# The first 256 of 512 rows of x transposed by TensorE, the other 256 by a DMA transpose, with the first four groups of h computed in two halves

## The chip, the cores and the metric

The kernel runs on one core of a Trainium2 chip. The time is device microseconds from launch to end. The record also has each launch's span, from the first to the last instruction: most launches take 1.7 to 2 us more than it. One number is the median of several launches. Launches of one kernel differ by up to about a microsecond (in one of the jobs below, 11 launches of the same kernel lay between 320.51 and 321.78, their spans between 318.7 and 319.8), and the whole effect in question here is smaller than that. So much of the evidence is taken from single traces, by the place of single instructions.

## The reference

```python
# x: (1, 2048, 640), w1: (640, 1536), w2: (1536, 640), grad_out like x; all bfloat16
def forward(x, w1, w2):
    h = jnp.einsum("bsd,df->bsf", x, w1)
    h = jax.nn.silu(h)
    return jnp.einsum("bsf,fd->bsd", h, w2)
# outputs: the forward result and the gradients for x, w1 and w2
```

## The kernel before

The kernel goes through x in four chunks of 512 rows. For each chunk it computes h in 12 groups: a group is 128 columns of h, made by five matmuls (one for each 128 of the 640 columns of x) of 128 x 128 weights by 512 columns. Then come the output product, the product for grad_out and the gradient of x, and at the end the gradients of the weights. Only the head of the program, up to about 20 us, is touched by the change. There x must be transposed first: TensorE does it against an identity matrix, and VectorE and ScalarE copy the results out of PSUM.

```python
KM, NWARM, LAG_G = 2, 22, 4     # P = 128, SC = FC = 512, DT = 5, FT = 12, FB = 4, NFC = 3
...
for i in range(NWARM):          # keeps TensorE busy until x has landed
    early.append(nc.tensor.matmul(wp[:, 0:P], lhsT=warm[:], rhs=warm[:], start=True, stop=True))
...
early += [load_x_half(0), load_x_half(1), load_w1_rows(0, 1), load_w1_rows(1, KM)]
load_w1_rows(KM, DT)            # w1 rows of columns 0..511: "the first slice"
...
for fc in range(1, NFC):
    load_w1(fc * FC, (fc + 1) * FC)     # second and third slice, 640 KB each
...
nc.sync.dma_start(out=w2_nat[:], in_=w2_v[:])
goT_next = load_goT(0)                  # a DMA transpose

def pe_x_half(xT, half):
    lo = half * 2 * P
    for dt_ in range(DT):
        tp = ps_h.tile([P, 2, P], dt_in, name="tp", tag="hp")
        for q in range(2):
            nc.tensor.transpose(tp[:, q, :], x_two[:, half, q, dt_ * P:(dt_ + 1) * P], ident[:])
        copy = nc.scalar.copy if dt_ % 2 else nc.vector.tensor_copy
        copy(out=xT[:, dt_, lo:lo + 2 * P].rearrange("p (s q) -> p q s", q=2), in_=tp[:])

pe_x_half(xT_next, 0)
pe_x_half(xT_next, 1)
...
def h_first(xT, aT, ghT):       # the 12 groups of the first chunk
    hps = []
    for ft in range(FB):
        hps.append(ps_h.tile([P, SC], FP32, name="hp"))
    for dt_ in range(KM):
        for ft in range(FB):
            h_mm(hps[ft], ft, xT, dt_, dt_ + 1)
    for i in range(FT + LAG_G):
        if i < FT:
            if i < FB:
                h_mm(hps[i], i, xT, KM, DT)
            else:
                hps.append(ps_h.tile([P, SC], FP32, name="hp"))
                h_mm(hps[i], i, xT, 0, DT)
            silu_a(i, hps[i], aT)
        ...
```

All loads go through SyncE's one queue, in the order of the text. Groups 1 to 4 need the first w1 slice, groups 5 to 8 the second. I call the first group that needs the second slice "group 5".

## Time and profile before

| | before |
|---|---|
| median | 320.82 us (3 launches, 320.68 to 321.51) |
| span of the profiled launch | 319.4 us |
| TensorE (PE) busy | 314.6 us, 98% |
| transposes of x | 20, from 3.19 us, 107 ns apart |
| second w1 slice: issued, landed on the last engine | 2.48, 9.91 us |
| group 5's first matmul | 10.08 us |

First the line of engine times of the page of before: busy microseconds, share of the span, number of instructions.

```profile
PE 314.6 (98%) x1469; PEld 146.3 (46%) x1498; DVE 102.6 (32%) x182; ACT 77.9 (24%) x142; POOL 0.7 (0%) x6
```

PE has almost no idle time, so whatever the head saves or loses moves the end by as much. Next the timeline of before: PE from 3 to 12 us, then PEld (the weight loads) over the same stretch. The columns are start, length of the merged piece, engine, line, operation, tiles, shape and count; in brackets the idle time ahead and what ended it.

```profile
3.19 2.31 PE L197 MATMUL tp<-ident,x_two 128*128 128x128 bf16 x20 [0.16 <-DMA x_two<-in_x_dram]
5.30 6.02 PE L206 MATMUL hp<-xT,w_nat 128*128 128x512 bf16 x24
```

```profile
6.15 3.60 PEld L206 LDWEIGHTS <-w_nat 128*128 128x128 bf16 x17 [0.28 <-issue]
9.95 1.95 PEld L206 LDWEIGHTS <-w_nat 128*128 128x128 bf16 x10 [0.21 <-DMA w_nat<-in_w_dram]
```

PE has no break between the transposes and the twelfth microsecond. But the weight load at 9.95 is group 5's, and it waited 0.21 us for the second w1 slice. It waits ahead of its matmul, so PE itself lost nothing; yet the slice had only about 0.1 us to spare. Last the queue of SyncE (SPq) in the timeline of before (here the length is how long SyncE was busy issuing), and from the DMA view of 0 to 20 us the moved GB/s, a number for each half microsecond.

```profile
0.09 0.87 SPq L173 DMA_DIRECT2D x_two<-in_x_dram  x2
1.00 1.44 SPq L178 DMA_DIRECT2D w_nat<-in_w_dram  x3
2.48 1.06 SPq L169 DMA_DIRECT2D w_nat<-in_w_dram  x2
```

```profile
GB/s 0 0 82 266 374 374 351 366 289 358 358 336 324 324 348 371 374 379 376 380 366 366 358 364 364 364 366 344 271 133 62 26 23 83 292 289 319 152 28 39
```

The two w1 slices (L169) are issued at 2.48 us. From 2 to 14 us the queue moves about 350 GB/s almost without a gap.

### The profile page before, as it was taken

How to read it: one execution, taken by the hardware profiler on the slowest of the kernel's cores; microseconds unless marked ns; L12 is line 12 of the kernel's file. 1: busy time of each engine (PE TensorE's matmuls, PEld its weight loads, DVE VectorE, ACT ScalarE, POOL GpSimd, SP SyncE). 2: the span in 40 equal slices, each digit the busy share in tenths (PEclk: the TensorE clock that was granted, in tenths of full speed). 3: DMA queues.
4: the chain of work that ended last, by engine and by line, in shares of the span. 5: the costliest groups of instructions: out<-in, count | busy, mean ns of one | idle time of the engine just before them, and what ended most of it. 6: DMA issues, size and time to landing. Idle time of an engine off the chain costs nothing.

```text
span 319.4 us, 3541 instructions
## 1 busy us (share of the span) xinstructions
PE 314.6 (98%) x1469; PEld 146.3 (46%) x1498; DVE 102.6 (32%) x182; ACT 77.9 (24%) x142; POOL 0.7 (0%) x6
## 2 busy tenths in 40 slices
PE   9999999999999999999999999999999999999996
PEld 6444444444444444444444444444444444444443
DVE  3771541477410087710147741000000100001001
ACT  4960000545201254411054520110100001001100
POOL 0000000000000000000000000000000000000000
PEclk9999999999999999999999999999999999999999
DMA  8999999999999855292634079819999998995111
GB/s 282 307 180 222 246 292 264 341 263 292 293 278 271 223 190 140 86 308 76 171 114 133 2 259 267 217 30 294 265 212 257 267 240 292 253 294 182 49 37 45
DMA packets 147312, 67.33 MB, mean 211 GB/s; under 512 B 112609, under 2 KB 147041, under 8 KB 147297
## 3 DMA queue, kind: packets, MB, share of 16 engines
q1 hardware_dynamic: 147296, 67.12, 80.9%
q8 instruction: 11, 0.18, 0.2%
q14 instruction: 5, 0.03, 0.0%
HBM read 9.83 MB, written 28.97 MB: 121 GB/s over the span
## 4 chain that ended last, share of the span: by engine, by line
PE 98%; DMA 1%; issue 1%; DVE 0%; DVEq 0%; SPq 0%
PE hp L269 32%; PE hp L206 16%; PE hp L357 16%; PE hp L253 16%; PE hp L406 15%; PE hp L387 1%; DMA x_two<-in_x_dram 1%; PE tp L197 1%; DVE g L398 0%; DVEq L398 0%; SPq L434 0%
## 5 line engine op out<-in xcount | busy, mean ns | idle before, releaser
L206 PE MATMUL hp<-xT,w_nat 128*128 128x512 bf16 x238 | 57.2, 381 | 0.1
L253 PE MATMUL hp<-goT,w2T 128*128 128x512 bf16 x232 | 56.4, 379 | 0.4
L269 PE MATMUL hp<-aT,w_nat 128*128 128x512 bf16 x235 | 52.2, 379 | 0.3
L269 PE MATMUL hp<-ghT,w1T 128*128 128x512 bf16 x235 | 52.2, 379 | 0.3
L357 PE MATMUL hp<-a_blk,go_nat 128*128 128x512 bf16 x236 | 51.8, 379 | 0.2
L406 PE MATMUL hp<-gh_blk,x_nat 128*128 128x512 bf16 x219 | 48.2, 379 | 0.3
L277 ACT ACTIVATE oT<-hp 128x512 bf16<-128x512 f32 x24 | 14.3, 598 | 109.8 <-PE hp L269 109.8
L215 ACT ACTIVATE aT<-hp 128x512 bf16<-128x512 f32 x48 | 29.9, 625 | 33.0 <-PE hp L206 33.0
L206 PEld LDWEIGHTS <-w_nat 128*128 128x128 bf16 x240 | 23.6, 99 | 28.4 <-issue 0.6
L269 PEld LDWEIGHTS <-w1T 128*128 128x128 bf16 x240 | 23.5, 98 | 28.3
L357 PEld LDWEIGHTS <-go_nat 128*128 128x128 bf16 x240 | 23.5, 98 | 28.3
L253 PEld LDWEIGHTS <-w2T 128*128 128x128 bf16 x240 | 23.5, 98 | 28.3
L269 PEld LDWEIGHTS <-w_nat 128*128 128x128 bf16 x240 | 23.5, 98 | 28.4
L279 DVE CAST oT<-hp 128x512 bf16<-128x512 f32 x16 | 11.1, 692 | 77.0 <-PE hp L269 63.5
L260 DVE SCALAR_TENSOR_TENSOR ghT<-ghT,hp 128x512 bf16<-128x512 bf16 x48 | 32.5, 682 | 7.3 <-PE hp L253 7.3
L406 PEld LDWEIGHTS <-x_nat 128*128 128x128 bf16 x224 | 21.9, 98 | 26.4
L222 DVE SCALAR_TENSOR_TENSOR ghT<-aT,v 128x512 bf16<-128x512 bf16 x48 | 32.8, 687 | 0.5
L221 DVE TENSOR_SCALAR v<-t 128x512 bf16<-128x512 f32 x48 | 20.3, 426 | 30.5 <-ACT t L219 30.5
L219 ACT ACTIVATE t<-hp 128x512 f32<-128x512 f32 x48 | 29.8, 625 | 0.0
L417 DVE CAST g<-hp 128x512 bf16<-128x512 f32 x7 | 4.8, 692 | 47.0 <-PE hp L406 27.4
L367 DVE CAST g2T<-hp 128x512 bf16<-128x512 f32 x7 | 4.8, 692 | 46.1 <-PE hp L357 46.1
L365 ACT ACTIVATE g2T<-hp 128x512 bf16<-128x512 f32 x8 | 4.8, 597 | 47.0 <-PE hp L357 40.8
(20 smaller groups left out, 27.0 us busy)
## 6 DMA issues: line engine op xcount, KB each, us to landing
aT_scr<-aT SPq DMA_DIRECT2D x4, 1536.0 KB, 6.2
ghT_scr<-ghT SPq DMA_DIRECT2D x4, 1536.0 KB, 8.0
out_dram<-o_sb SPq DMA_DIRECT2D x8, 640.0 KB, 3.6
oT_scr<-oT SPq DMA_DIRECT2D x4, 640.0 KB, 3.6
go_nat<-in_grad_out_dram SPq DMA_DIRECT2D x4, 640.0 KB, 6.4
x_nat<-in_x_dram SPq DMA_DIRECT2D x4, 640.0 KB, 5.3
gxT_scr<-oT SPq DMA_DIRECT2D x4, 640.0 KB, 4.7
w_nat<-in_w_dram SPq DMA_DIRECT2D x1, 1920.0 KB, 13.4
```

The lines of the kernel that those rows point to most:

```text
L206: nc.tensor.matmul(hp[:], lhsT=w1_nat[:, dt_, ft * P:(ft + 1) * P], rhs=xT[:, dt_, :], start=(dt_ == 0), stop=(dt_ == DT - 1),)
L215: nc.scalar.activation(aT[:, ft, :], hp[:], ACT.Silu)
L219: nc.scalar.activation(t[:], hp[:], ACT.Tanh, scale=0.5)
L221: nc.vector.tensor_scalar(out=v[:], in0=t[:], scalar1=-0.5, scalar2=0.5, op0=ALU.mult, op1=ALU.add)
L222: nc.vector.scalar_tensor_tensor(out=ghT[:, ft, :], in0=aT[:, ft, :], scalar=1.0, in1=v[:], op0=ALU.subtract, op1=ALU.mult)
L253: nc.tensor.matmul(gp[:], lhsT=w2T[:, dt_, ft * P:(ft + 1) * P], rhs=goT[:, dt_, :], start=(dt_ == 0), stop=(dt_ == DT - 1),)
L260: nc.vector.scalar_tensor_tensor(out=ghT[:, ft, :], in0=ghT[:, ft, :], scalar=1.0, in1=gp[:], op0=ALU.add, op1=ALU.mult)
L269: nc.tensor.matmul(op_[:], lhsT=w_all[:, ft, dt_ * P:(dt_ + 1) * P], rhs=rhs_all[:, ft, :], start=(ft == 0), stop=(ft == FT - 1),)
L277: nc.scalar.activation(oT[:, dt_, :], op_[:], ACT.Copy)
L279: nc.vector.tensor_copy(out=oT[:, dt_, :], in_=op_[:])
L357: nc.tensor.matmul(gp[:], lhsT=go_nat[:, st, dt_ * P:(dt_ + 1) * P], rhs=a_blk[:, st, :], start=(st == 0), stop=(st == ST - 1),)
L406: nc.tensor.matmul(gp[:], lhsT=x_nat[:, st, dt_ * P:(dt_ + 1) * P], rhs=gh_blk[:, st, :], start=(st == 0), stop=(st == ST - 1),)
```

## The change

The intent is to start h earlier. Half of the transposes go away from PE. The first four groups begin on the 256 rows that PE has transposed. The other 256 rows come transposed by the DMA, behind the first w1 slice, while PE works on the first half.

```diff
-    KM = 2
-    NWARM = 22
+    NWARM = 24
+    HC = 2 * P
...
-        early += [load_x_half(0), load_x_half(1), load_w1_rows(0, 1), load_w1_rows(1, KM)]
-        load_w1_rows(KM, DT)
+        early += load_x() + [load_w1_rows(0, 1), load_w1_rows(1, 3)]      # load_x: the first 256 rows
+        load_w1_rows(3, DT)
+        nc.sync.dma_start_transpose(out=xT_next[:, :, HC:SC], in_=x2[HC:SC, :])
         start_before_entry_wait(nc, {i.ins.name for i in early})
         for fc in range(1, NFC):
             load_w1(fc * FC, (fc + 1) * FC)
...
-        pe_x_half(xT_next, 0)
-        pe_x_half(xT_next, 1)
+        for dt_ in range(DT):
+            tp = ps_h.tile([P, 2, P], dt_in, name="tp", tag="hp")
+            for q in range(2):
+                nc.tensor.transpose(tp[:, q, :], x_two[:, q, dt_ * P:(dt_ + 1) * P], ident[:])
+            ...                                # one copy into xT_next[:, dt_, 0:HC]
...
-            for dt_ in range(KM):
+            for dt_ in range(DT):
                 for ft in range(FB):
-                    h_mm(hps[ft], ft, xT, dt_, dt_ + 1)
+                    h_mm(hps[ft], ft, xT, dt_, dt_ + 1, slice(0, HC))
...
                     if i < FB:
-                        h_mm(hps[i], i, xT, KM, DT)
+                        h_mm(hps[i], i, xT, 0, DT, slice(HC, SC))
```

More of the change, by code (lines that the diff above doesn't have):

```diff
@@ L165, with load_x @@
         xT_next = xpool.tile([P, DT, SC], dt_in, name="xT")
-        x_two = cpool.tile([P, 2, 2, D], dt_in, name="x_two")
+        x_two = cpool.tile([P, 2, D], dt_in, name="x_two")
         def load_w1(lo, hi):
             nc.sync.dma_start(out=w1_nat[:, :, lo:hi], in_=w1_v[:, :, lo:hi])
-        def load_x_half(half):
-            lo = half * 2 * P
-            return nc.sync.dma_start(
-                out=x_two[:, half, :, :], in_=x2[lo:lo + 2 * P, :].rearrange("(p q) d -> p q d", q=2)
-            )
+        def load_x():
+            return [nc.sync.dma_start(out=x_two[:], in_=x2[0:HC, :].rearrange("(p q) d -> p q d", q=2))]
         def load_w1_rows(lo, hi):
             return nc.sync.dma_start(out=w1_nat[:, lo:hi, 0:FC], in_=w1_v[:, lo:hi, 0:FC])
-        early += [load_x_half(0), load_x_half(1), load_w1_rows(0, 1), load_w1_rows(1, KM)]
-        load_w1_rows(KM, DT)
+        early += load_x() + [load_w1_rows(0, 1), load_w1_rows(1, 3)]
+        load_w1_rows(3, DT)
+        nc.sync.dma_start_transpose(out=xT_next[:, :, HC:SC], in_=x2[HC:SC, :])
         start_before_entry_wait(nc, {i.ins.name for i in early})
@@ L190, with h_mm @@
         nc.sync.dma_start_transpose(out=w1T[:], in_=w1[:, :])
-        def pe_x_half(xT, half):
-            lo = half * 2 * P
-            for dt_ in range(DT):
-                tp = ps_h.tile([P, 2, P], dt_in, name="tp", tag="hp")
-                for q in range(2):
-                    nc.tensor.transpose(tp[:, q, :], x_two[:, half, q, dt_ * P:(dt_ + 1) * P], ident[:])
-                copy = nc.scalar.copy if dt_ % 2 else nc.vector.tensor_copy
-                copy(out=xT[:, dt_, lo:lo + 2 * P].rearrange("p (s q) -> p q s", q=2), in_=tp[:])
-        pe_x_half(xT_next, 0)
-        pe_x_half(xT_next, 1)
-        def h_mm(hp, ft, xT, lo, hi):
+        for dt_ in range(DT):
+            tp = ps_h.tile([P, 2, P], dt_in, name="tp", tag="hp")
+            for q in range(2):
+                nc.tensor.transpose(tp[:, q, :], x_two[:, q, dt_ * P:(dt_ + 1) * P], ident[:])
+            copy_tp = nc.scalar.copy if dt_ % 2 else nc.vector.tensor_copy
+            copy_tp(out=xT_next[:, dt_, 0:HC], in_=tp[:].rearrange("p q s -> p s q"))
+        def h_mm(hp, ft, xT, lo, hi, cols=slice(0, SC)):
             for dt_ in range(lo, hi):
                 nc.tensor.matmul(
-                    hp[:],
+                    hp[:, cols],
                     lhsT=w1_nat[:, dt_, ft * P:(ft + 1) * P],
-                    rhs=xT[:, dt_, :],
+                    rhs=xT[:, dt_, cols],
                     start=(dt_ == 0),
```

## The prediction

> **What bounds the kernel.** TensorE. On the profile's first part PE is busy 314.6 of 319.4 us, and the waits of PE sum to 0.7 us. So only the head can move: whatever the first groups of h gain or lose reaches the end one for one.
>
> **The head before (timeline and single PE records).** x's first half lands at 3.14 us (DMA part of the chain). Twenty 128-column transposes follow, 107 ns apart, 3.19 to 5.30. The first three 512-column matmuls are 419, 427 and 260 ns apart, all later ones 216: the granted clock is half until 6.22 us. The Trainium skill, "TensorE: Matmul & The Clock Gate", Part 1, says that the array starts at half clock and is released after some 3.4 us of activity; this trace agrees in kind (release at 6.22). Group 5, the first that needs the second w1 slice, starts at 10.08; that slice's last engine landed at 9.91. So PE sets the head, but the slice has only 0.1 us to spare.
>
> **What the change does to PE.** It removes ten transposes (10 x 107 ns at half clock) and five copies, and cuts 20 matmuls of 512 columns into 40 of 256, which I estimate at 213 ns cold and 110 warm, from 427 and 216. Estimated walk: transposes 3.19 to 4.26, nine cold half matmuls to 6.22, eleven warm ones to 7.41, twenty on the second half to 9.61. Group 5 could start at 9.61 instead of 10.08: at most 0.47 us. The removed transposes ran at half clock, and the release doesn't come sooner, so their 1.07 us are worth only half. NWARM 24 fills 0.2 us before x lands and moves nothing.
>
> **What it does to the queue.** x's second 320 KB now come by a DMA transpose behind the w1 rows and ahead of w1 slice 1. goT's transpose shows how these behave: packets of the fast engines stood up to 2.7 us until the slowest engine had finished w2_nat (17.0 us), and SyncE's issue lasted 12.1 us, ending 0.2 us after that. At full rate its packets move at about 285 GB/s, against 365 for plain loads. The w1 rows, which ended at 6.51, should end near 5.6; plus 320 KB at 285 GB/s gives a landing at 6.9 to 7.5, about when the second halves want it (7.4). The later slices are issued behind it (from about 5.8 rather than 2.5), 1.2 us pass from issue to first packet, and 640 KB take 1.9: slice 1 lands at 9.0 to 10.5, against a need at 9.61. I expect this wait to eat about half of the gain. Slice 2 (need 13.9) and w2_nat (need 18.3, landed at 17.0) keep slack.
>
> **Predicted.** 320.6 us, range 319.9 to 322.0. Faster by over 2%: 1%; within 2%: 98%; slower by over 2%: 1%.
>
> **What would show it right.** Transposes end near 4.3; half matmuls are 213, then 110 ns apart; the second halves start at 7.4 to 7.6; the transpose of x lands near 7; its issue takes over 2 us; group 5 waits for slice 1's DMA by 0 to 0.7 us; from the second slice on, everything is as before, shifted by under half a microsecond.
>
> **What would make it wrong.** The transpose may be held by a straggling engine, or start slowly, and land at 8.5 or later: then PE waits at the second halves and at slice 1, a loss of about 1 us. A wait before 6.22 us could put off the clock's release. If the release comes at another time in this launch, the gain is up to 1 us, or smaller.

## The result, and the profile after

The changed kernel takes 321.09 us (median of 4, 321.02 to 321.14), against 320.77 us (4, 320.68 to 321.51). The ratio is 1.0005, with a 95% interval of 0.9987 to 1.0022: the same. Ratios here and below are the mean time of one kernel's fast runs over that of the other's fast runs of the same rounds, so they are not quite the ratio of the medians quoted. A second job gave 321.22 against 321.23 us, ratio 1.0003.

The line of engine times of the page of after:

```profile
PE 314.0 (98%) x1481; PEld 147.2 (46%) x1510; DVE 101.1 (32%) x179; ACT 77.1 (24%) x140; POOL 0.7 (0%) x6
```

PE does have less to do (314.0 us for 314.6). The timeline of PE from 3 to 12 us shows where that went:

```profile
3.29 1.25 PE L193 MATMUL tp<-ident,x_two 128*128 128x128 bf16 x10
4.33 5.02 PE L199 MATMUL hp<-xT,w_nat 128*128 128x256 bf16 x40
9.88 2.33 PE L199 MATMUL hp<-xT,w_nat 128*128 128x512 bf16 x9 [0.53 <-DMA w_nat<-in_w_dram]
```

h begins 0.97 us sooner (4.33 for 5.30). The forty half matmuls run without a break; the last starts at 9.08, and the next should have followed 0.11 us later. It started at 9.88, so PE stood 0.69 us by its starts. (The profile counts 0.53, because it models the end of the matmul before, which is pipelined.) The chain of waits of after names what it waited for:

```profile
1.57 0.38 SPq L175
...
1.99 1.86 SPq L179
...
3.90 5.94 DMA w_nat<-in_w_dram
...
9.88 0.39 PE hp L199
```

By this chain the end of the program now hangs on SyncE's queue: on the issue of the last w1 rows (L175), of the DMA transpose (L179, 1.86 us), then on the second slice, issued at 3.90 and landed 5.94 us later, at 9.83. The GB/s line of the DMA view of after, again 0 to 20 us in half microseconds:

```profile
GB/s 0 0 133 251 348 241 223 238 319 285 217 289 276 236 307 326 367 332 350 362 356 366 364 369 361 356 364 364 389 343 324 244 99 76 159 290 290 291 109 98
```

From 2.5 to 7 us the queue moves 217 to 319 GB/s, where before it moved 289 to 374. The same bytes stand ahead of the second slice as before (320 KB of x as plain load or transpose, the rest unchanged), so it lands no earlier, though PE now wants it earlier.

### The profile page after: what moved, and what is told of

It reads as the page before. It is cut to its first block, busy times and chain, and to the rows that moved or that the text cites. A ratio compares the mean times of both kernels' runs of the same rounds, so it can differ in the third digit from the quotient of the medians.

```text
span 319.2 us, 3567 instructions
## 1 busy us (share of the span) xinstructions
PE 314.0 (98%) x1481; PEld 147.2 (46%) x1510; DVE 101.1 (32%) x179; ACT 77.1 (24%) x140; POOL 0.7 (0%) x6
## 4 chain that ended last, share of the span: by engine, by line
PE 96%; DMA 2%; SPq 1%; issue 1%; DVE 0%; DVEq 0%
PE hp L262 32%; PE hp L246 16%; PE hp L350 16%; PE hp L399 15%; PE hp L199 15%; DMA w_nat<-in_w_dram 2%; PE hp L380 1%; SPq L179 1%; SPq L175 0%; DVE g L391 0%; DVEq L391 0%
## 5 line engine op out<-in xcount | busy, mean ns | idle before, releaser
L199 PE MATMUL hp<-xT,w_nat 128*128 128x512 bf16 (+1 forms) x252 | 57.2, 365 | 0.9 <-DMA w_nat<-in_w_dram 0.5
L199 PEld LDWEIGHTS <-w_nat 128*128 128x128 bf16 x260 | 25.6, 99 | 27.3 <-DMA w_nat<-in_w_dram 0.8
L208 ACT ACTIVATE aT<-hp 128x512 bf16<-128x512 f32 x48 | 28.7, 604 | 33.4 <-PE hp L199 33.4
L262 PEld LDWEIGHTS <-w_nat 128*128 128x128 bf16 x240 | 23.5, 98 | 28.3
L212 ACT ACTIVATE t<-hp 128x512 f32<-128x512 f32 x48 | 28.6, 601 | 0.0
```

The lines of the kernel that those rows point to most:

```text
L199: nc.tensor.matmul(hp[:, cols], lhsT=w1_nat[:, dt_, ft * P:(ft + 1) * P], rhs=xT[:, dt_, cols], start=(dt_ == 0), stop=(dt_ == DT - 1),)
L208: nc.scalar.activation(aT[:, ft, :], hp[:], ACT.Silu)
L212: nc.scalar.activation(t[:], hp[:], ACT.Tanh, scale=0.5)
L262: nc.tensor.matmul(op_[:], lhsT=w_all[:, ft, dt_ * P:(dt_ + 1) * P], rhs=rhs_all[:, ft, :], start=(ft == 0), stop=(ft == FT - 1),)
```

## The experiments

Twelve runs followed. The traces of before, after and eight of these runs give the places below; g1, g2, g3 and e4 come in their own sections. The places are read from single instruction and semaphore records. "clock" is when the granted clock went from half to full, "-" where the trace has no record. "slice" is the landing of the second w1 slice on the ninth of 16 engines, and on the last. "stood" is PE's start-to-start gap at group 5 beyond the usual one. "next stage" is the first weight load of the output product, that is, where the head ends.

```
                    clock  first tp  slice 9th/last  group 5 stood  next stage  span
before              6.22   3.19      7.35 /  9.91        0.0          18.50     319.4
c1 before           -      2.86*     7.95 /  9.73        0.0          18.44     319.4
after               5.33   3.29      8.67 /  9.83        0.69         18.31     319.2
c2 after            6.27   3.04      8.90 / 10.53        1.04         19.01     319.9
e1 before, reuse    6.71   3.29      7.87 /  8.48        0.0          18.79     319.7
e2 after, reuse     6.51   3.11      8.70 /  9.93        0.0          18.09     319.0
e3 after, plain     4.42   3.17      8.06 /  9.21        0.0          19.15     320.1
c3 after, split     -      3.26      9.84 / 10.75**      0.0          18.59***  319.3
h1 after, split     4.39   3.16      9.17 /  9.89**      0.0          17.86***  318.6
c4 before, split    5.85   3.18      7.81 /  8.46**      0.0          18.30     319.2
*   a pause followed: x's second half landed at 4.63; the transposes were 107 ns
    apart before the pause and 56 after it
**  both halves; the first, which group 5 needs: c3 8.75 / 9.65, h1 8.11 / 8.67,
    c4 6.74 / 7.38
*** this weight load waited for w2 (landed at 18.55 and 17.82); PE did not wait,
    so go by the span
```

Behind "next stage" nothing differs: in the eight rows without *** the span ends 300.9 us after it.

### Both kernels once more

No edit. The first pair of traces differed in the moment at which the clock was released, so each kernel was profiled a second time.

> The kernel before, unchanged, as a control. Ratio 1.000 within 0.1%. It also gives a second trace of the same code. If the moment at which the granted clock is released differs from launch to launch, this trace will not release at 6.22 us again; if it releases near 5.3 us, the theory (the second w1 slice's landing sets the head) expects group 5 to wait for that slice by some 0.3 us and to start near 9.9 all the same. The rival (PE's own work sets the head) expects group 5 near 9.6 without a wait.

> The changed kernel, unchanged. Theory (the slice's landing sets the head in it): group 5 again starts right behind the landing of the second w1 slice, 9.5 to 10.3 us, after a wait of PE of 0.3 us or more, and its times scatter little; ratio to before 1.000 to 1.002. Rival (the first trace's release of the clock at 5.33 us was luck): with a later release the wait is gone and the time grows by up to 0.5 us.

Before again: 320.96 us, ratio 0.9997. After again: 321.22 us, ratio 1.0003. The second trace of before has no clock record, but its transposes show full clock after the pause, so it was released by about 4.7 us. It still settles nothing about an early release, because late data held PE up (x for 0.8 us, w1 rows for 0.2); group 5's weight load came at 9.81 there and PE lost nothing at it. The second trace of after settles more. This is its PE timeline:

```profile
4.11 5.59 PE L199 MATMUL hp<-xT,w_nat 128*128 128x256 bf16 x40
10.58 1.69 PE L199 MATMUL hp<-xT,w_nat 128*128 128x512 bf16 x7 [0.88 <-DMA w_nat<-in_w_dram]
```

Its clock was released at 6.27 us, practically where the first trace of before has it (6.22), so the two can be compared directly. Without the wait group 5 would have started at 9.54 (the last half matmul at 9.43 and 0.11 us more), against 10.08 in before. That is 0.54 us, of which about 0.08 comes from x landing 0.15 us earlier at half clock. So the predicted saving of PE, 0.47 us, is there almost to the hundredth. Then PE stood 1.04 us for the slice, and the next stage began 0.51 us later than in before. The rival, for which a later release makes the wait go away, is refuted by this trace: with a later release the wait was longer, because the slice too came later. The first trace of after must be read with its clock in mind. Its release was 0.89 us earlier than that of before, worth about 0.44 us (an estimate, half of it), so at the clock of before group 5 would have been due near 9.6 and the wait would have been about 0.3 us, not 0.69. Its next stage began 0.19 us sooner than in before. So the wait took more than half of the gain in one trace, and all of it and 0.5 us more in the other.

### Taking the wait away with other data (wrong on purpose)

```diff
-                        h_mm(hps[i], i, xT, 0, DT)
+                        h_mm(hps[i], i - FB if i < 2 * FB else i, xT, 0, DT)
```

Groups 5 to 8 of the first chunk use the first slice's columns again. Their results are wrong (relative error 0.41), the matmuls have the same shapes, and the second slice is still loaded.

> Wrong on purpose: the kernel before, with groups 5 to 8 of the first chunk taking the first w1 slice's columns again, so that no matmul before group 9 waits for the second slice; its load stays where it was. Both theories: before hardly waits for that slice, so group 5 starts at 9.6 to 10.1 us depending on when the clock is released, and the time stays within 0.1% of before.

> Wrong on purpose: the changed kernel with the same reuse of the first slice's columns. Theory (the wait for the second slice takes back the change's gain): with that wait gone group 5 starts at 9.2 to 9.7 us instead of 9.9 and 10.6, 0.3 to 0.6 us ahead of the same edit of before at the same release of the clock, and the time is 0.1 to 0.2% below it. Rival (the change gains nothing on PE, because the 256-column matmuls or a later wait cost as much): group 5 starts within 0.1 us of the same edit of before, and so does the end.

Before with reuse took 321.19 us, ratio 1.0002 (0.9989 to 1.0015). After with reuse took 320.71 us, ratio 0.9992 (0.9980 to 1.0004). The intervals overlap, but these ratios are to before. Set against each other, the spans of after with reuse (five launches, 318.8 to 319.1, mean 318.92) are shorter than those of before with reuse (five, 318.9 to 319.7, mean 319.28) and of before in the same job (eleven, 318.9 to 319.7, mean 319.24; the difference of 0.32 is over three times its standard error). The traces say the same thing. The PE timeline of after with reuse goes through group 5 without a break:

```profile
3.11 1.25 PE L193 MATMUL tp<-ident,x_two 128*128 128x128 bf16 x10
4.15 8.06 PE L199 MATMUL hp<-xT,w_nat 128*128 128x256 bf16 x51
```

and so does that of before with reuse:

```profile
3.29 2.32 PE L197 MATMUL tp<-ident,x_two 128*128 128x128 bf16 x20 [0.26 <-DMA x_two<-in_x_dram]
5.40 6.86 PE L206 MATMUL hp<-xT,w_nat 128*128 128x512 bf16 x28
```

Group 5's first weight load comes at 9.57 in the one and 10.15 in the other, its first matmul at 9.67 and 10.37, and the next stage starts at 18.09 against 18.79. Of these 0.69 us, the earlier clock (0.20 us, worth half) and the earlier x (0.18 us, worth half) explain about 0.2; about 0.5 is left, the size of the gain on PE. So with the wait gone the change does gain, and nothing later takes it back. The rival, that the change gains nothing on PE, falls.

### The second slice in two halves

```diff
-        for fc in range(1, NFC):
-            load_w1(fc * FC, (fc + 1) * FC)
+        load_w1(FC, FC + 2 * P)
+        load_w1(FC + 2 * P, 2 * FC)
+        load_w1(2 * FC, 3 * FC)
```

This is the honest way to take that wait away: group 5 needs only the first half.

> The changed kernel with the second w1 slice loaded in two DMAs of 256 columns instead of one of 512, same place in the queue. Theory (slice wait ate the gain): group 5 needs only the first 320 KB, which land about 0.9 us sooner; PE's wait of 0.5 us before group 5 is gone or under 0.2 us and the time falls by 0.4 to 0.7 us, ratio to before about 0.999. Rival (the loss lies later in the queue or in the 256-column matmuls): the wait moves or goes and the time stays within 0.1 us of the changed kernel's.

> The kernel before with the same split of the second w1 slice. Theory: before is at the slice's edge too (0.1 us to spare with the late clock, short by 0.3 us with an early one), so it gains 0 to 0.4 us, less than the changed kernel gains by the same edit. Rival (PE's work sets the head of before): no change, ratio 1.000.

> The changed kernel with the second slice in two halves, once more, for a second sample of its time and trace. If the first result (0.999 of before, interval 0.9976 to 1.0005) was a real gain, the ratio is again 0.998 to 0.9995 and the trace shows no wait of PE at group 5. If it was the launches' scatter, the ratio is 1.000 or above. In the trace, PE's waits before group 5 (rows or the transpose landing late, 0.75 and 0.42 us the first time) decide which.

After with the split: 320.83 us against 321.23, ratio 0.9990 (0.9976 to 1.0005); the second time 320.66 against 321.01, ratio 0.9992 (0.9978 to 1.0006). Before with the split: 321.11 against 321.23, ratio 0.9998. In both traces of after with the split PE did not stand at group 5. In the first it stood earlier instead, about 0.75 us for w1 rows and 0.4 for the DMA transpose, which landed late (7.69 us). In the second it stood 0.3 us for rows and 0.3 for the transpose, and with a clock released at 4.39 it gave the shortest span of all, 318.6. This is its PE timeline from 4.2 us, without a gap at group 5 (by starts, 0.11 us from the last half matmul to the next; the view merges short gaps, so the two stops of 0.3 us don't show either):

```profile
4.20 8.02 PE L200 MATMUL hp<-xT,w_nat 128*128 128x256 bf16 x52
```

So the split after gained 0.4 and 0.35 us of median in two jobs, of the predicted size, but each interval holds 1.0. Part of that is not the kernel's: in the first job three launches of before took 2.5 to 2.9 us beyond their span. By mean span the gain is 0.12 us there (319.04 against 319.16), about what before gained by the same split (319.07), and 0.26 in the second (318.88 against 319.14). It is the best version seen that computes the right result, and it is not shown to beat before.

### A plain load in place of the DMA transpose

```diff
-        nc.sync.dma_start_transpose(out=xT_next[:, :, HC:SC], in_=x2[HC:SC, :])
+        nc.sync.dma_start(out=x_sec[:], in_=x2[HC:SC, :].rearrange("(p q) d -> p q d", q=2))
```

Ten transposes by PE and five copies for `x_sec` stand ahead of the first half's last four matmuls.

> The changed kernel, but x's second 256 rows come by a plain load at the same place of the queue and are transposed by TensorE within the first half's matmuls. It tells what the DMA transpose itself costs the queue. Theory A (the transpose slows the queue: w1 rows at about 230 GB/s while it is issued, troughs before and after its packets): rows move at 320 GB/s or more, and the second slice lands 0.5 us or more ahead of the changed kernel's 9.8 to 10.5, at 8.5 to 9.7. Rival B (smaller first loads and straggling engines do it, whatever follows): the second slice lands at 9.5 or later again. The time: ten transposes at full clock cost about 0.6 to 0.8 us of PE, so 0 to 0.1% over before.

321.83 us, ratio 1.0025 (1.0013 to 1.0037), so 0.8 us slower, more than expected: PE waited for `x_sec` and for rows too. The queue is what it was built for, and both theories got half. The GB/s line of its DMA view of 0 to 20 us:

```profile
GB/s 0 0 159 289 365 241 244 207 248 307 327 309 317 333 373 315 289 340 383 357 329 368 389 387 384 369 386 353 358 336 241 120 42 61 288 292 289 191 124 114
```

The queue still moved only 205 to 270 GB/s (by quarter microseconds) between 2.5 and 4.25 us, when the w1 rows were in it, with no transpose near, so that slow stretch is not the transpose's doing, and Theory A's 320 GB/s was wrong. But the second slice was on nine engines at 8.06 us, against 8.67 to 8.90 with the transpose and 7.35 to 7.95 before, and on the last at 9.21. In this one trace, then, the transpose costs the slice some 0.6 to 0.8 us, and the rest, 0.1 to 0.7 us, would be the order's with its smaller first load. SyncE could also issue the slice at 2.49 us instead of 3.90 to 4.47, as issuing the plain load took 0.47 us and the transpose 1.86 to 2.44. How much of the transpose's cost is this late issue and how much its packets, no run separates.

### The DMA transpose behind the second slice

```diff
-        nc.sync.dma_start_transpose(...)          # ahead of the loop
-        for fc in range(1, NFC):
-            load_w1(fc * FC, (fc + 1) * FC)
+        load_w1(FC, 2 * FC)
+        nc.sync.dma_start_transpose(...)
+        load_w1(2 * FC, 3 * FC)
```

> The changed kernel with the DMA transpose of x issued behind the second w1 slice instead of ahead of it. Theory A (the transpose holds up the queue): the second slice lands at 8.0 to 8.8 us and group 5 waits for nothing, but the second halves wait for x until 8.8 to 10 us, 1.5 us or more after the first halves end, so the time is 0.2 to 0.5% above the changed kernel's. Rival B (slice late for another reason): the slice lands as late as before, near 9.8.

323.36 us, ratio 1.0085 (1.0069 to 1.0101). Its PE timeline:

```profile
7.05 1.05 PE L199 MATMUL hp<-xT,w_nat 128*128 128x256 bf16 x8 [1.06 <-DMA w_nat<-in_w_dram]
10.02 4.29 PE L199 MATMUL hp<-xT,w_nat 128*128 128x256 bf16 x29 [1.92 <-DMA xT<-in_x_dram]
```

The slice landed at 8.71 us, as Theory A has it, and group 5 did not wait. But 320 KB less stood ahead of it here, so this alone does not tell a transpose from a plain load. The second halves waited 1.9 us for x, which landed at 9.97. The loss is larger than expected, because the last w1 rows also came late (7.01 us, against 5.47 to 6.38 in five traces with the transpose next behind them) though their place in the queue had not changed. Why, no run shows.

### The slices on ScalarE's queue

```diff
+        for lo, hi in ((FC, 2 * FC), (2 * FC, 3 * FC)):
+            nc.scalar.activation(w1_nat[:, 0, lo:lo + 1], warm[:, 0:1], ACT.Silu)   # holds the issue to 2.26 us
+            nc.scalar.dma_start(out=w1_nat[:, :, lo:hi], in_=w1_v[:, :, lo:hi])
```

The second run has the split second slice too.

> The changed kernel, but w1 slices 1 and 2 are issued from ScalarE's queue (right after its table load, near 2.3 us) instead of behind the DMA transpose on SyncE's. Theory (in SyncE's queue the slice stands behind a transpose that leaves the DMA engines idle before and after its packets): the slice lands at 7.5 to 9.2 us, in the gaps; group 5's wait is gone; the transpose of x lands somewhat later (7 to 8 us) and may cost a wait of up to 0.6 us; time 0 to 0.2% below the changed kernel. Rival (the engines' bandwidth is the limit, not the order): the slice comes earlier only by making the w1 rows and the transpose later by as much, PE waits there instead, time as the changed kernel's or worse.

> The same with the second slice in two halves of 256 columns. Theory: its first half lands at 6 to 8 us; no wait at group 5; time within 0.1% of the run with the whole slice on ScalarE's queue, and at or below the changed kernel with the split on SyncE's queue (0.999 of before). Rival: as for the run before.

Both expectations missed by far. 327.12 us, ratio 1.0189 (1.0168 to 1.0211); with the split 324.87 us, ratio 1.0148 (1.0116 to 1.0180). The PE timeline of the run with the whole slice:

```profile
5.11 1.93 PE L199 MATMUL hp<-xT,w_nat 128*128 128x256 bf16 x16 [0.43 <-DMA w_nat<-in_w_dram]
10.87 5.46 PE L199 MATMUL hp<-xT,w_nat 128*128 128x256 bf16 x28 [3.83 <-DMA xT<-in_x_dram]
```

The DMA transpose, which in five traces with nothing on the other queue landed at 6.71 to 7.69 us, landed at 10.83 with plain loads of another queue beside it, and with the split at 10.25. The Trainium skill, "DMA: Bandwidth & Descriptors", section "Issuing engines are not separate DMA queues", says that DMAs from different engines run on the same 16 DMA engines and interleave; this run agrees, and in it the transpose paid most: it came 3 to 4 us later, while the slice, expected at 7.5 to 9.2 us, landed at 11.39, against 9.83 and 10.53 in the two traces of after. PE stood long enough to lose its clock as well. In the stretches of that run (columns: stretch, length, busy time of each engine, granted clock PEclk, DMA share, GB/s):

```profile
7.00:10.30 3.30, 0.04 (x1) 0.00 (x0) 0.00 (x0) 0.00 (x0) 0.00 (x0) 1.00 1.09 278
10.30:13.80 3.50, 2.93 (x15) 2.08 (x15) 0.51 (x2) 1.66 (x3) 0.00 (x0) 0.51 1.09 350
```

PE's matmuls started at 6.77 us and then at 10.87, and the granted clock was half from 10.34 to 13.75. With the split PE stood 2.9 us at this place and kept its full clock.

### The first slice's rows in one DMA

```diff
-        early += load_x() + [load_w1_rows(0, 1), load_w1_rows(1, 3)]
-        load_w1_rows(3, DT)
+        early += load_x() + [load_w1_rows(0, 1), load_w1_rows(1, DT)]
```

This stands on top of the split, to see whether many small DMAs starve the engines near 3 us.

> The changed kernel with the split slice and with w1 rows 1 to 4 in one DMA of 512 KB instead of two of 256 KB. In all runs of the changed kernel's order the rows moved at 180 to 270 GB/s near 2.5 to 4.0 us with 10 to 14 of 16 engines at work. If many small DMAs in a row starve the engines, the rows move at 300 GB/s or more here and land by 5.0 us, and the time is 0.1% below the split alone. If it is something else about that early moment, the rate stays below 270 GB/s, and as the first rows are now waited for with the last, PE waits up to 1 us near 5 us.

321.24 us against 320.84, ratio 1.0016 (0.9999 to 1.0033). The queue moved 193 to 311 GB/s between 2.5 and 3.75 us, the rows were there at 6.04, and PE stood about 1.1 us for them, until 6.08 us. Neither branch fits wholly: the rate passed 270 GB/s for a while, but the rows did not land by 5.0. What starves the engines there stays open.

## Why the prediction was right, and where it was off

The measured 321.09 us lies in the predicted range (319.9 to 322.0), and "within 2%" holds. The middle, 320.6, was too low: it meant a gain of about 0.2 us, and no gain was measured in two jobs (ratios 1.0005 and 1.0003, though both intervals would hold one of 0.2 us).

- **PE's saving: right.** Half matmuls were 213 ns apart at half clock and 109 to 110 at full clock, transposes ended near 4.3 us, and at equal clock the walk to group 5 was shorter by 0.54 us, 0.08 of it luck, against 0.47 predicted.
- **The clock sets what a removed cold instruction is worth: right, with wide play.** The release came between 3.51 and 6.71 us over the traces that record it, and each microsecond of it is worth half a microsecond of PE's work, as much as the whole change.
- **The w1 rows and the DMA transpose's landing: right.** The rows landed at 5.63 and 5.47 us, predicted near 5.6, though the queue was slower than the 365 GB/s reckoned with; the transpose at 6.91 and 6.71, predicted 6.9 to 7.5. **Its issue: partly.** 1.86 and 2.44 us, predicted over 2; but it did not hold SyncE until the queue was nearly empty (slice issued at 3.90 and 4.47, predicted 5.8).
- **The step that was off: "I expect this wait to eat about half of the gain."** The kind of wait and its place were right. The slice landed at 9.83 and 10.53 us, the one near the middle and the other at the edge of the predicted 9.0 to 10.5. At the clock of before the wait takes about 0.3 us with the first landing, more than half of the gain, and 1.04 us with the second, all of it and 0.5 us more. The sum behind it (5.8 + 1.2 + 1.9 = 8.9 us) fits the landing on the ninth engine, 8.67 and 8.90, partly by luck: the slice's issue was 1.3 to 1.9 us earlier than reckoned, and its way from there to the ninth engine 1.3 to 1.7 us longer. What the sum has no term for is the time from the ninth engine to the last, 1.16 and 1.63 us. The change did not make this lag: it was 2.56, 1.78 and 0.61 us in the three traces of the order of before, with 15 of 16 engines there at 8.23 us in the first of them and the last at 9.91.
- **Nothing later: right.** After group 5 both kernels run alike, and with the wait taken away the gain stays to the end (e2: 320.71 us against e1: 321.19).

That the wait for the second slice takes the gain back is shown by the edit that takes it away with other data, in the traces and in the spans of all launches; the split points the same way within noise. That the transpose itself delays the slice rests on one trace and the landing times in it. Why the rows are slow near 3 us, and why some engines lag, is not settled.

## What to carry to other kernels

Before taking work off a busy engine, look for the next thing it will want and how long that has already been there: here a weight load with 0.1 us to spare turned 0.5 us of saved work into waiting. A load that several consumers share in turn can be cut so that the first of them needs only its own part. A DMA transpose in a full queue can cost more than its bytes (here, in one trace, 0.6 to 0.8 us of what stood behind it), and one that shares the DMA engines with plain loads of another queue can come late (here 3 to 4 us).

## What the Trainium skill lacked or had wrong

- "Advanced Engine Details and Errata", section "X-Bar Transpose (TRN2)", says that "TRN2 transpose DMAs are as fast as regular DMAs" and expects 350 to 400 GB/s. Here transposes moved 285 to 295 GB/s while they flowed, plain loads 350 to 375, and just before and after that flow the rate fell (to 154 and 172 GB/s for a quarter microsecond in the first trace of after, to 128 and 12 in the second).
- The same section and "DMA: Bandwidth & Descriptors" lack that packets of a transpose can stand until the slowest engine is done with the load ahead. In before, packets of the transpose of grad_out stood up to 2.69 us. They ended at 16.86 to 16.91 us, as the plain load ahead was landing (16.95 to 17.01), and from 15.5 to 16.75 us the queue moved 16 to 26 GB/s, about one engine's sixteenth of 360 (an estimate from the rates above).
- "DMA: Bandwidth & Descriptors", section "Rules for kernel authors", says that a transpose next to ordinary DMAs "needs nothing". That is meant of correct results, and they were correct here. It lacks the cost in time: the transpose landed at 10.83 us instead of 6.71 to 7.69 with two plain loads on ScalarE's queue.
- "TensorE: Matmul & The Clock Gate", section "Back-to-back issue gap", gives about 131 ns for each matmul of a stream of weight loads and 512-column matmuls. Here they were 216 ns apart at full clock, and 109 to 110 with 256 columns.
- The same page, Part 1, calls the clock's window free-running and 3413 ns long. That agrees: in the run that lost its clock the half clock lasted from 10.340 to 13.754 us, 3.41 us, and the release came between 3.51 and 6.71 us from launch to launch, 3.2 us apart, so that it can outweigh a change of this size.
- No page says by how much time a bulk load's last engines lag. Here, in loads of 640 KB from SyncE's queue, it was 0.7 to 1.1 us for four of 16 in the first trace of after (8.70 on the twelfth, 9.40 to 9.83 on the last four), and 1.7 us for a single one in before (8.23 and 9.91).
